# Two orders on VectorE in the first block: when a weight tile's low part is made, and where the ELU's maximum stands

## The chip, the cores and the metric

The kernel runs on one core of a Trainium2 chip. The metric is the device time of one execution in microseconds. The engines speak of themselves as in the profile: PE is the tensor engine's matmuls, PEld its weight loads, DVE is VectorE, ACT is ScalarE, POOL is GpSimd, SP is SyncE, which here issues nearly all transfers.

## The reference

Inputs: q, k, v of 4 x 8 heads x 768 tokens x 64, eight memory keys and values per head, and six weight matrices, handed over as 64-bit floats in two 32-bit words each.

```python
for each chunk of 32 queries:                     # keys: 8 of memory, 16 left, 32 own, 8 right
    scores = (q_c @ k_full.T) / sqrt(64)
    a = exp(scores - max(scores)); a = a / (sum(a) + 1e-9)
    out[chunk] = a @ v_full
x = out as 3072 tokens x 512
h = x @ w_in                                      # 512 -> 2048
g = where(h > 0, h, exp(min(h, 0)) - 1)           # ELU
x = g @ w_out                                     # 2048 -> 512
a, b = x @ w1, x @ w2                             # 512 -> 1024 each
y = ((a * b) @ w3) @ w_out2                       # 1024 -> 1024 -> 512
```

## The kernel before, in words

The tokens are worked on in eight blocks of 384. Attention goes in 24 groups G of 128 queries, three to a block. The first layer and its ELU go in 16 tiles per block: n counts (block, tile), so n = 0 to 15 is the first block. Every large product is made of three matmuls on split operands: high x high, high x low, low x high (`mm3`, L123 to L126), where the high part is a rounded copy (ScalarE) and the low part the remainder (VectorE).

The first block carries more than the later ones: while it runs, the 32 weight tiles of w_in and w_out are brought in, converted and split for the first time. `Feed` does this, one job per weight tile, in steps. Step i issues, for different jobs:

- on ScalarE `hi_of` (L172, the high part of job i-2's tile) and `rebase` (L159, the first pass over the raw words of job i);
- on VectorE `shift` (L163) and `low` (L167) of job i-1, then `lo_of` (L175, the low part of job i-2's tile);
- on SyncE the loads of raw words for later jobs (L140, L148): there are four raw buffers, and four more for the first 16 jobs. A buffer comes free when `low` has read it.

The intermediate f tiles have four buffers, so `rebase` of job i writes where job i-4 was last read by `lo_of`. `until(i)` runs steps until job i is complete.

Five steps run before the loop (the `f` letters in START, between the attention of groups 0 to 2). Then iteration n < 16 issues in this order; each engine takes its own instructions in the order of issue (the schedule is written out by hand):

1. `mm_h(n)`: 12 matmuls into one of two banks that alternate with n; it must wait until `elu_max(n-2)` has read that bank.
2. `elu_hi(n-1)` (ScalarE, L559), a feed step, `elu_lo(n-1)` (VectorE, L563).
3. `at_step`: the attention work of slot 2n.
4. `elu_exp(n)`: two ScalarE passes (L549, L550).
5. `x()`: `mm_x(n-2)` (12 matmuls that read elu_lo's result), a feed step, `at_step` of slot 2n+1.
6. `elu_max(n)` (VectorE, L555).

A slot holds steps of a group's attention: turn (L305 to L317), scores (L329), max (L346, L347, then the exponential L348 on ScalarE), sum (L354 to L357), norm (L366, two instructions), flip (L377), values (L388), out (split, L120 on ScalarE and L121 on VectorE). For groups 3, 4 and 5 the odd slots that hold VectorE work are those of n = 2 and 7 (sum), 3 and 8 (flip), 4 and 9 (out), 12 (max) and 13 (norm).

The job order is w_in 0, 1, 2, then w_out and w_in in turn, so w_in tile n is job 2n-2 (n of 2 and more) and w_out tile n-2 is job 2n-1.

The functions that the diff touches, with their callers:

Of the kernel before, what the change touches and what calls it, by code (L numbers as in the profile page):

```python
# [19 lines left out]
def tile_kernel(  # L20
# [41 lines left out]
    FF1 = w_in.shape[1] // P  # L62
# [124 lines left out]
    class Feed:  # L187
# [16 lines left out]
        def step(self):  # L204
            i = self.at
            self.load(i + 1)
            if i - 2 == first_late:
                end_early()
            if 0 <= i - 2 < len(self.jobs):
                self.jobs[i - 2].to = W[self.jobs[i - 2].slot]  # L210
            self.do(i - 2, hi_of)
            self.do(i - 1, shift, low)
            self.do(i - 2, lo_of)
            self.do(i, rebase)
            self.at += 1
            self.load(max(min(i + RAWS + SPARE, SPARE_JOBS), i + RAWS))

        def until(self, i):
            while self.at - 3 < i:
                self.step()  # L220


# [306 lines left out]
    def at_step():  # L529
        store_next()  # L530
        for _, _, fn, arg in sorted(slots.pop(slot_at[0], ()), key=lambda x: x[:2]):
            fn(arg)
        slot_at[0] += 1
# [204 lines left out]
    with tc.manual_schedule():  # L738
        def weight(i):
            if i < FF1:  # L740
                return Job((raw_cols, w_in, i), slot=i)
            return Job((raw_rows, w_out, i - FF1, 0), slot=i)

        jobs, due = [], {}
        order = sorted(range(2 * FF1), key=lambda i: i if i < FF1 else i - FF1 + 2)
        for i in order:
            due[i] = len(jobs)
            jobs.append(weight(i))
        first_late = min(due[i] for i in LATER)
        feed = Feed(jobs)  # L750

        load_qk(0)
        make_identity(nc, ident)
        nc.gpsimd.memset(front, 0.0)
        nc.gpsimd.memset(vw[0:LEFT, 0], 0.0)
        for c in range(NCG):
            for s in range(2):
                nc.gpsimd.memset(odd[c * CH:(c + 1) * CH, s], float(c % 2 == s))
        feed.load(1)
        load_qk(1)  # L760
        feed.load(2)
        load_v(0)
        load_qk(2)
        load_v(1)
        feed.load(3)
        load_v(2)
        feed.load(5)
        one = dict(t=at_turn, u=at_first, s=at_scores, m=at_max, z=at_sum, n=at_norm, p=at_flip, v=at_values, o=at_out, k=load_qk, w=load_v)
        for what in START.split():
            if what == "f":  # L770
                feed.step()
            else:
                one[what[0]](int(what[1]))
        early_psum.close()
        psum_x = ctx.enter_context(tc.tile_pool(name="psum_x", bufs=1, space=PSUM))
        for i in range(KT):
            PS[i] = psum_x.tile([P, 512], F32, name=f"bank{i}")
        NH = NB * FF1
        for n in range(NH + 2):
            j, f, at, last = seq[n] if n < NH else (NB, n - NH, n - NH, False)  # L780
            first = at < 2 and n >= 2
            if j == NB - 1 and f == 0:
                store_next()
                mid_ctx.close()
                at_ctx.close()
                late = ctx.enter_context(tc.tile_pool(name="late", bufs=1, side="right"))
                more = [late.tile([P, 2, 2, TB], F32R, name=f"xc{i}") for i in range(3)]
                left.append({})
                for i, what in enumerate(LEFTS[:4]):
                    left[0][what] = [xhl[i // 2][:, r, i % 2 * 2:i % 2 * 2 + 2, :] for r in range(2)]  # L790
                for i, what in enumerate(LEFTS[4:]):
                    left[0][what] = [more[i][:, r] for r in range(2)]
            if n == FF1:
                feed.until(len(feed.jobs) - 1)
                raw_ctx.close()
                mid_ctx = ExitStack()
                pools["raw"] = mid_ctx.enter_context(tc.tile_pool(name="raw2", bufs=2, side="right"))
                pools["st"] = mid_ctx.enter_context(tc.tile_pool(name="st_p", bufs=2, side="right"))
                mid_load(2)

            def x():
                if n >= 2:
                    if n < FF1 + 2:
                        feed.until(due[FF1 + seq[n - 2][1]])
                    mm_x(n - 2)
                    if at == 1 and n < NH:
                        store_x1(j - 1)
                if n < FF1:
                    feed.step()
                at_step()  # L810

            if first:
                x()
            if n < NH:
                if j == 0:
                    feed.until(due[f])
                mm_h(n)
            spread = n < FF1
            if 1 <= n <= FF1:
                elu_hi(n - 1)  # L820
            if spread:
                feed.step()
            if 1 <= n <= FF1:
                elu_lo(n - 1)
            if n < NH and not spread:
                elu_exp(n)
            at_step()
            if spread:
                elu_exp(n)
            if FF1 < n < NH:  # L830
                elu_lo(n - 1)
            if not first:
                x()
            if n < NH:
                elu_max(n)
            if n < NH and not spread:
                elu_hi(n)
                if n == NH - 1:
                    elu_lo(n)
            if n >= NH - FF1:  # L840

                free = [f] if n < NH else []
                if n >= NH - FF1 + 2:
                    free.append(FF1 + n - 2 - (NH - FF1))
                for slot in free:
                    keep_free(slot)
            if j == NB - 1:
                if f == 4:
                    load_x1(0)
                if f == 8:  # L850
                    left_step(0, 0)
                if f == 10:
                    left_step(0, 1)
        store_x1(NB - 1)
        wq_places()
        load_wq(0, range(3))
        for i in range(2, len(LEFTS)):
            left_step(0, i)
        load_x1(1)
        for half in range(2):  # L860
            for c in range(FF2):
                for i in range(KT):
                    mm_wc(half, c, i)
                    if c == FF2 - 1:
                        keep_wc(half, i)
                if half:
                    if c == 0:
                        load_wq(0, [3])
                    if c in (1, 2, 3):
                        load_wq(1, [c - 1])  # L870
                    if c == 3:
                        load_wq(1, [3])
                    if c in (4, 5, 6):
                        load_wq(2, [c - 4])
                    if c == 7:
                        load_wq(2, [3])
        w_ctx.close()
        end = ctx.enter_context(tc.tile_pool(name="end", bufs=1))
        more = [end.tile([P, 2, 2, TB], F32R, name=f"xd{i}") for i in range(len(LEFTS))]
        left.append({what: [t[:, r] for r in range(2)] for what, t in zip(LEFTS, more)})  # L880
        e_f.update(enumerate([eg_p.tile([P, TB], F32, tag="eg", name="eg") for _ in range(2)] + [end.tile([P, TB], F32, name=f"e{i}") for i in range(4)]))
        gq.extend([g_p.tile([P, 2, TB], F32R, tag="g", name="g") for _ in range(3)] + [end.tile([P, 2, TB], F32R, name="g3")])
        NA = NPAIR * FF2
        for n in range(NA + 1):
            p, f = divmod(n, FF2)

            def behind(t, n=n, p=p, f=f):
                if t == 0 and n < NA and p + 1 < NPAIR and f >= 1:
                    left_step(p + 1, f - 1)
                if n >= 1:  # L890
                    mm_o(n - 1, t)

            def stored(t, p=p, f=f, n=n):
                if n >= 1 and f == 0:
                    store_out(p - 1, t)

            mm_step(n, n == NA, {t: lambda t=t: behind(t) for t in range(2 * GPB)}, stored)
            if n < NA:
                if p + 2 < NPAIR and f == FF2 - 1:
                    load_x1(p + 2)  # L900
                load_wq(n + FOLD)
# [30 lines left out]
```

## Time and profile before

| | |
|---|---|
| median of 3 runs | 1092.84 us (1092.37 to 1093.17) |
| the profiled execution | 1092.9 us, span 1091.1 us |
| PE, PEld busy, share of the span | 96%, 91% |
| DVE, ACT busy | 53%, 42% |
| mean granted clock of TensorE | 0.983 |
| transfers | 180.40 MB, 165 GB/s |

The shares are means over stages. The first block is roughly the stretch from 33 to 133 us; its 17th tile, n = 16, starts the second block. Matmuls are pipelined: the busy time of PE counts ends that are modelled, and the start-to-start distance says how fast it goes. In a timeline row the first number is the start in us from the span's start, the second the duration; the bracket at the end gives the idle time before the instruction and what ended it.

### The profile page before, as it was taken

Reading aid. Unit: us, or ns where it says so; the run is one execution under the profiler, and the core shown is the slowest. Engines: PE = TensorE matmul, PEld = TensorE weight load, DVE = VectorE, ACT = ScalarE, POOL = GpSimd, SP = SyncE. Lnnn points to the kernel's source line nnn. Section 1 sums busy time; section 2 is a strip of 40 time slices with the busy share of each in tenths; the row PEclk is TensorE's granted clock in tenths of the full one; section 3 lists DMA queues with packets and bytes.
Section 4 is the critical chain, followed back from the end, with each engine's and each line's share of the span. In section 5 each row is a group of like instructions: output and inputs, shape, how many; then the busy total and the mean of one; then the engine's idle time right before and its main releaser. Section 6 shows DMA issues by size and latency. Waiting matters only on the chain.

```text
span 1091.1 us, 20849 instructions
## 1 busy us (share of the span) xinstructions
PE 1049.1 (96%) x8528; PEld 991.6 (91%) x8528; DVE 581.9 (53%) x1080; ACT 458.5 (42%) x965; POOL 1.7 (0%) x16
## 2 busy tenths in 40 slices
PE   4788899999999999999999999999999999999998
PEld 3688899999999999999999999789999999999997
DVE  4898656666566567665565334134443444443333
ACT  3676455455555455555454443022232223222222
POOL 0000000000000000000000000000000000000000
PEclk8799999999999999999999999999999999999999
DMA  8956356555454466455351765455466466555521
GB/s 193 299 142 189 99 152 176 154 168 163 144 169 134 137 177 187 126 162 172 105 155 44 244 245 172 137 182 169 143 212 234 155 211 223 156 170 186 186 85 58
DMA packets 170090, 180.40 MB, mean 165 GB/s; under 512 B 101388, under 2 KB 140300, under 8 KB 169996
## 3 DMA queue, kind: packets, MB, share of 16 engines
q1 hardware_dynamic: 168956, 178.81, 53.5%
q8 instruction: 67, 1.10, 0.4%
q10 hardware_dynamic: 1040, 0.26, 0.1%
q14 instruction: 27, 0.22, 0.1%
HBM read 139.20 MB, written 39.85 MB: 164 GB/s over the span
## 4 chain that ended last, share of the span: by engine, by line
PE 86%; DVE 6%; ACT 5%; issue 1%; DMA 1%; SPq 0%; ACTq 0%; DVEq 0%
PE bank L124 18%; PE bank L125 18%; PE bank L126 18%; PE bank L672 7%; PE bank L673 7%; PE bank L671 7%; PE banks L388 2%; PE banks L126 2%; PE banks L125 2%; PE banks L124 2%; PE banks L329 1%; DVE w L175 1%; PE banks L305 1%; ACT w L172 1%; ACT f L159 1%
## 5 line engine op out<-in xcount | busy, mean ns | idle before, releaser
L124 PE MATMUL bank<-xhl,w 128*128 128x384 f32 x512 | 178.2, 348 | 10.6 <-DVE eg L555 9.8
L124 PE MATMUL bank<-g,w 128*128 128x384 f32 x512 | 175.7, 343 | 0.0
L125 PE MATMUL bank<-xhl,w 128*128 128x384 f32 x512 | 173.8, 339 | 0.9 <-DVE xhl L121 0.9
L126 PE MATMUL bank<-xhl,w 128*128 128x384 f32 x512 | 173.8, 339 | 0.0
L125 PE MATMUL bank<-g,w 128*128 128x384 f32 x512 | 171.7, 335 | 0.0
L126 PE MATMUL bank<-g,w 128*128 128x384 f32 x512 | 171.6, 335 | 0.0
L559 ACT CAST g<-eg 128x384 fp32r<-128x384 f32 x128 | 66.1, 517 | 111.9 <-DVE eg L555 111.5
L124 PEld LDWEIGHTS bank<-xhl,w 128*128 128x128 f32 x512 | 97.6, 191 | 14.7 <-DVE eg L555 11.5
L555 DVE SCALAR_TENSOR_TENSOR eg<-eg,bank 128x384 f32<-128x384 f32 x128 | 70.1, 548 | 55.7 <-ACT eg L550 55.7
L455 DVE TENSOR_TENSOR e<-bank,e 128x384 f32<-128x384 f32 x64 | 35.7, 558 | 118.9 <-PE bank L673 76.6
L125 PEld LDWEIGHTS bank<-xhl,w 128*128 128x128 f32 x512 | 97.9, 191 | 1.3 <-DVE xhl L121 1.3
L549 ACT ACTIVATE eg<-bank 128x384 f32<-128x384 f32 x128 | 62.8, 491 | 85.1 <-PE bank L126 85.0
L126 PEld LDWEIGHTS bank<-xhl,w 128*128 128x128 f32 x512 | 97.9, 191 | 0.0
L124 PEld LDWEIGHTS bank<-g,w 128*128 128x128 f32 x512 | 96.6, 189 | 1.1
L125 PEld LDWEIGHTS bank<-g,w 128*128 128x128 f32 x512 | 96.7, 189 | 0.2 <-DVE g L563 0.2
L126 PEld LDWEIGHTS bank<-g,w 128*128 128x128 f32 x512 | 96.4, 188 | 0.0
L719 ACT CAST g<-e 128x384 fp32r<-128x384 f32 x64 | 29.7, 511 | 145.7 <-DVE e L455 145.7
L563 DVE TENSOR_TENSOR g<-eg,g 128x384 fp32r<-128x384 f32 x128 | 70.7, 552 | 16.9 <-ACT g L559 16.9
L672 PE MATMUL bank<-xd,w 128*128 128x384 f32 x224 | 75.8, 338 | 0.0
L673 PE MATMUL bank<-xd,w 128*128 128x384 f32 x224 | 75.6, 337 | 0.0
L671 PE MATMUL bank<-xd,w 128*128 128x384 f32 x224 | 74.9, 334 | 0.0
L550 ACT ACTIVATE eg<-eg 128x384 f32<-128x384 f32 x128 | 67.3, 526 | 4.1
(141 smaller groups left out, 1824.2 us busy)
## 6 DMA issues: line engine op xcount, KB each, us to landing
w<-wqd SPq DMA_DIRECT2D x96, 512.0 KB
raw<-in_moe_w_dram SPq DMA_DIRECT2D x32, 512.0 KB
wqd<-st SPq DMA_DIRECT2D x24, 512.0 KB
raw<-in_moe_w_out_dram SPq DMA_DIRECT2D x20, 512.0 KB
w3d<-st SPq DMA_DIRECT2D x16, 512.0 KB
w<-w3d SPq DMA_DIRECT2D x16, 512.0 KB
w<-wqd SPq DMA_DIRECT2D x32, 256.0 KB
raw<-in_moe_w_in_dram SPq DMA_DIRECT2D x12, 512.0 KB
```

The costliest lines, as they stand in the source:

```text
L124: mm(o, lhsT=w_hi, rhs=x_hi, start=start, stop=False)
L125: mm(o, lhsT=w_hi, rhs=x_lo, start=False, stop=False)
L126: mm(o, lhsT=w_lo, rhs=x_hi, start=False, stop=stop)
L455: nc.vector.tensor_tensor(out=o, in0=a, in1=b, op=op)
L549: nc.scalar.activation(e, h_t[n], AF.Relu, scale=-1.0)
L550: nc.scalar.activation(e, e, AF.Exp, scale=-1.0)
L555: nc.vector.scalar_tensor_tensor(out=e, in0=e, scalar=-1.0, in1=h_t.pop(n), op0=ALU.add, op1=ALU.max)
L559: nc.scalar.copy(g_t[n][:, 0, :], eg_t[n])
L563: nc.vector.tensor_tensor(out=g[:, 1, :], in0=eg_t.pop(n), in1=g[:, 0, :].bitcast(F32), op=ALU.subtract)
L671: mm(o, lhsT=args[0], rhs=args[2], start=start and i == 0, stop=False, skip_group_check=more)
L672: mm(o, lhsT=args[0], rhs=args[3], start=False, stop=False, skip_group_check=more)
L673: mm(o, lhsT=args[1], rhs=args[2], start=False, stop=i == 1, skip_group_check=more)
```

## The change

In the feed, the low part of a weight tile is issued one step later than before, and ahead of `shift` and `low` instead of behind them; `until` counts one step more. In the loop, for n < 16, `elu_max(n)` is issued inside `x()`, between the feed step and the attention of slot 2n+1, instead of after it. For n of 16 and more nothing changes.

```diff
@@ Feed.step
             self.do(i - 2, hi_of)
+            self.do(i - 3, lo_of)
             self.do(i - 1, shift, low)
-            self.do(i - 2, lo_of)
             self.do(i, rebase)
@@ Feed.until
-            while self.at - 3 < i:
+            while self.at - 4 < i:
                 self.step()
@@ x(), in the loop over n
                 if n < FF1:
                     feed.step()
+                    elu_max(n)
                 at_step()
@@ the end of an iteration
             if not first:
                 x()
-            if n < NH:
+            if FF1 <= n < NH:
                 elu_max(n)
```

## Rows read from the trace of the kernel before

**Rows 1.** Busy time of each engine, 42 to 124 us (windows view).

```profile
42.00:124.00 82.00, 69.84 (x667) 66.02 (x666) 71.80 (x135) 56.46 (x118) 0.00 (x0) 0.95 0.61 174
```

**Rows 2.** Waits of VectorE, 42 to 124 us (total us, times, longest).

```profile
DVE w L175 <- ACT w L172: 7.0, 7, 1.4
DVE xhl L121 <- ACT xhl L120: 0.5, 2, 0.2
```

**Rows 3.** The tensor engine's waits for the maximum, 42 to 124 us (same view).

```profile
PE bank L124 <- DVE eg L555: 9.8, 4, 3.1
```

**Rows 4.** VectorE's groups by line, 42 to 124 us: the maximum.

```profile
L555 DVE SCALAR_TENSOR_TENSOR eg<-eg,bank 128x384 f32<-128x384 f32 x14 | 7.6, 542 | 0.0
```

**Rows 5.** VectorE in order of time, 109 to 126 us (start, us; idle before).

```profile
109.00 0.69 DVE L175 TENSOR_TENSOR w<-f,w 128x512 fp32r<-128x512 f32 x1 [1.42 <-ACT w L172]
...
120.07 0.69 DVE L167 SCALAR_TENSOR_TENSOR f<-raw,f 128x512 int32<-128x512 int32 x1
120.68 0.68 DVE L175 TENSOR_TENSOR w<-f,w 128x512 fp32r<-128x512 f32 x1
121.28 1.29 DVE L366 TENSOR_TENSOR e<-e,rc 128x512 f32<-128x512 f32 x2
122.48 0.55 DVE L555 SCALAR_TENSOR_TENSOR eg<-eg,bank 128x384 f32<-128x384 f32 x1
...
124.74 0.55 DVE L563 TENSOR_TENSOR g<-eg,g 128x384 fp32r<-128x384 f32 x1
125.21 1.24 DVE L377 STREAM_TRANSPOSE pT<-e 128x1024 f32<-128x1024 f32 x1
```

**Rows 6.** The tensor engine in order of time, 123 to 133 us.

```profile
123.08 0.57 PE L124 MATMUL bank<-xhl,w 128*128 128x384 f32 x1 [2.38 <-DVE eg L555]
...
126.93 1.16 PE L388 MATMUL banks<-pT,vw 64*64 64x64 f32 x64
...
132.73 0.44 PE L124 MATMUL bank<-xhl,w 128*128 128x384 f32 x1
```

**Rows 7.** The tensor engine's largest wait from 133 us to the end.

```profile
PE banks L305 <- DVE st L175: 2.2, 6, 0.4
```

**Rows 8.** VectorE in order of time, iterations 0 to 2.

```profile
43.12 0.69 DVE L175 TENSOR_TENSOR w<-f,w 128x512 fp32r<-128x512 f32 x1 [1.14 <-ACT w L172]
...
46.38 0.69 DVE L175 TENSOR_TENSOR w<-f,w 128x512 fp32r<-128x512 f32 x1 [1.05 <-ACT w L172]
...
50.05 0.69 DVE L167 SCALAR_TENSOR_TENSOR f<-raw,f 128x512 int32<-128x512 int32 x1
50.78 0.69 DVE L175 TENSOR_TENSOR w<-f,w 128x512 fp32r<-128x512 f32 x1
...
56.08 0.68 DVE L354 TENSOR_REDUCE sm<-e 128x8 f32<-128x512 f32 x1
...
57.33 0.55 DVE L555 SCALAR_TENSOR_TENSOR eg<-eg,bank 128x384 f32<-128x384 f32 x1
```

**Rows 9.** ScalarE in order of time, iterations 0 to 2.

```profile
42.05 0.52 ACT L550 ACTIVATE eg<-eg 128x384 f32<-128x384 f32 x1
42.48 0.60 ACT L172 CAST w<-f 128x512 fp32r<-128x512 f32 x1
...
45.30 0.54 ACT L559 CAST g<-eg 128x384 fp32r<-128x384 f32 x1
45.71 0.64 ACT L172 CAST w<-f 128x512 fp32r<-128x512 f32 x1
...
54.40 0.52 ACT L550 ACTIVATE eg<-eg 128x384 f32<-128x384 f32 x1
```

**Rows 10.** SyncE issues the raw tile of job 24.

```profile
88.94 0.37 SPq L140 DMA_DIRECT2D raw<-in_moe_w_in_dram  x1
```

**Rows 11.** ScalarE reads that tile.

```profile
97.53 0.67 ACT L159 ACTIVATE f<-raw 128x512 f32<-128x512 f32 x1
```

**Rows 12.** One raw tile's transfer, from the chain of waits (start, us).

```profile
59.01 3.29 DMA raw<-in_moe_w_in_dram
```
## The prediction

> **What bounds the kernel now.** I read the page first: over the whole span the tensor engine is busy nearly throughout, VectorE half of the time. That mean hides the first block, so the second view was the table of windows over 42 to 124 us, in which the feed of weights runs. There VectorE is busy 71.80 of 82.00 us and has the highest share of the engines [rows 1]. Third, the waits: in this stretch VectorE stands still 7.0 us, in 7 places, for the high part of a weight tile (w L172) before it can make the low part (w L175), and 0.5 us for attention's high part [rows 2]; the tensor engine stands still 9.8 us, in 4 places, for the maximum (eg L555) [rows 3]. The maximum itself never waited: idle before its 14 instructions is 0.0 [rows 4]. So the chain is: VectorE goes through its list in order, loses time at low parts whose high parts are late, and arrives late at elu_max; the next-but-one mm_h, which needs that bank, is late by as much. The last of these places is the hinge: elu_max(13) starts at 122.48 [rows 5], mm_h(15) starts right after it at 123.08, after 2.38 us of waiting [rows 6]. From there to mm_h(16) at 132.73 the tensor engine hardly pauses, and from 133 us to the end its largest wait adds up to 2.2 us, in pieces of 0.4 at most [rows 7]. What mm_h(15) gains is therefore not taken back later by an idle tensor engine: nothing downstream has a time of its own to wait for.
>
> **The sum: how much earlier is elu_max(13)?** I count what stands ahead of it on VectorE, before and after.
>
> *The waits for the high part.* After the change the low part in step i belongs to job i-3, whose high part was issued one step before; it finds it done. The 7 waits go: 7.0 us [rows 2]. Beside them are small delays below the resolution of that view: where nothing delays it, L175 starts 0.61 us after L167 (120.07 and 120.68, [rows 5]); in the second step of an iteration the two are 0.73 apart (50.05 and 50.78, [rows 8]), and I counted ten such pairs in the stretch: 10 x 0.12 = 1.2 us. The 0.5 us at attention's out [rows 2] stand in slots of n = 4 and 9, where elu_max (0.54 us, [rows 4]) now comes first and fills them.
>
> *What moves behind it.* In iteration 13 the odd slot holds norm, two instructions that take 1.20 us from start to start (121.28 to 122.48, [rows 5]); elu_max(13) now goes ahead of them. And with the low part one step later, one L175 fewer has been issued by then: 0.60 us (120.68 to 121.28, [rows 5]).
>
> Together 7.0 + 1.2 + 0.5 + 1.20 + 0.60 = 10.5 us.
>
> *What waits instead.* Behind the first seven places stands, in the new order, an instruction that also needs ScalarE: elu_max needs L550, elu_lo needs L559. Each of these sits one instruction ahead of the high part on ScalarE (L550 42.05, L172 42.48: 0.43; L559 45.30, L172 45.71: 0.41, [rows 9]), and the old job's low part, now in front, fills 0.60 more. So of a wait w about w - 1.03 is left: 0.11 of 1.14, 0.02 of 1.05 [rows 8], 0.39 of 1.42 [rows 5], and 0.7 over all seven. This holds while ScalarE keeps its distance to VectorE. Where it does not, the rest is larger: at 46.38 ScalarE comes from mm_h(0) and the copies of a turn. mm_h(0) starts some 0.6 us earlier (one low part fewer stands ahead of attention's last out before the loop), while VectorE has by then gained 1.14, so that about 0.5 us stays. There are three turns in the block; with half of that at the two others I take 0.7 + 0.8 = 1.5 us. The bounds: 0 if ScalarE follows wholly; 4.0 if the three turns keep their waits (1.05 [rows 8], 1.42 [rows 5] and a like one of 0.94) and 0.6 of the others stays. I stay nearer to the low end, because ScalarE is busy only 56.46 of 82 us [rows 1] and is itself mostly waiting for the maximum.
>
> elu_max(13) and mm_h(15) are earlier by 10.5 - 1.5 = 9.0 us.
>
> *Behind the hinge.* mm_h(15) is followed by the values of group 5 (L388). Before, they started at 126.93, which is 4.45 after elu_max(13) began and right behind mm_h(15)'s matmuls [rows 5, 6]. After, flip is late next: from elu_max's start 0.46 for it, norm 1.20, one low part 0.60, elu_lo 0.47 (124.74 to 125.21), flip 1.24 [rows 5], so 4.0 in all. If mm_h(15) runs as slowly as before (3.85 us up to the values, [rows 6]) the values start 4.45 after as well, otherwise up to 0.45 earlier. I take 0.2. Sum: 9.0 + 0.2 = 9.2 us.
>
> **Edits that I cost at nothing.** *Weights that are complete one step later.* mm_h(n) reads job 2n-2, whose low part is now made in step 2n+1; it waits anyway for elu_max(n-2), issued behind step 2n+2. mm_x(n-2) reads job 2n-1, made in step 2n+2, and waits anyway for elu_lo(n-2), behind step 2n+3. Neither can become the later one. *f tiles held one step longer.* rebase of job i now needs the low part of step i-1; but it stands behind the high part of job i-2, and that needs `low` of the same step, which VectorE makes after that low part. *until* asks for 35 steps at n = 16, and 37 have been issued. *SyncE* keeps its order; its raw loads wait for `low`, and come earlier with it.
>
> **The wait that is added.** elu_max(n) now stands ahead of attention's VectorE work in iterations 2, 3, 7, 8, 12 and 13, and that work, the next low part, shift and low stand behind its wait for L550; scores and values on the tensor engine wait for them. In iteration 2 L550 ended at 54.92 [rows 9] and elu_max began at 57.33 [rows 8]: 2.4 us of room, of which the move takes the 1.25 us that sum stood ahead of it (from 56.08, [rows 8]). 1.15 us is left, so I cost it at 0 beyond the rest above.
>
> One more look at whether VectorE's waits can be won back at all. The gaps of about 1.1 us in front of L175 [rows 8] stand beside pairs of the same kind that follow in 0.61 [rows 5], so a wait on another engine comes on top of the instructions' own pace. The Trainium skill speaks against the change here: VectorE: DVE Perf Modes, "The DRAIN you can't avoid", says that the flush behind each instruction sets the pace, and that taking out the semaphores between chained instructions saved nothing in its measurement. By that rule the sum would be 0, since the number of instructions stays; the trace does not agree where the awaited engine is another one.
>
> **The rivals.**
>
> *A. ScalarE takes over.* If the low part in front does not help, because VectorE arrives early by what it gained, then only the 0.43 of each wait goes: 7.0 - 7 x 0.43 = 4.0 stays, and so do the ten small delays and the 0.5. The gain is 10.5 - 4.0 - 1.7 = 4.8, the time 1088.1. For it: the same ScalarE list serves both. Against: its room above.
>
> *B. The number of instructions sets VectorE's pace.* 135 start in 82.00 us [rows 1], 0.607 each, about what L175 takes where nothing delays it; the change leaves their number as it is. Then the gaps would reappear elsewhere, and the time would be 1092.9. Against: the gaps stand at one kind of instruction only, and the maximum, which needs ScalarE too, has none [rows 4].
>
> *C. The raw tiles come too late.* Job 24's was issued at 88.94 [rows 10] and read at 97.53 [rows 11], 8.6 us later; one transfer took 3.29 [rows 12]. A pace that is faster by 9.2 of 82 us leaves 7.6. If transfers took over 8 us under load, jobs 16 to 31 would keep the old pace, half of the gain would go: about 1088.3. Against: 3.29.
>
> *D. Slower.* elu_max stops VectorE in front of attention. It decides from the point at which L550 comes more than 1.15 us later, relative to VectorE, than before. At 3.2 us later in all six iterations 6 x 2.05 = 12.3 us are lost against 10.5 gained: 1094.7. For it: VectorE gains time that ScalarE has to follow. Against: no idle time at all before the maximum so far [rows 4].
>
> **How the numbers follow.** The profiled execution took 1092.9 us (span 1091.1), 0.06 above the median of the runs, which I neglect. 1092.9 - 9.2 = 1083.7. Chances: forecast 0.72 (its own range 1082.3 to 1085.6: 7.3 to 10.6 gained, from a rest of 0 to 3.4), A 0.14, B 0.05, C 0.04, D 0.05. The range 1082.0 to 1088.4 takes in the forecast, A and C and leaves out B, D and the tails. Faster by over 0.2% (what a measurement can tell from no change): forecast, A and C, 0.90; within it B, 0.05; slower D, 0.05.
>
> **What would show it.** Right: in the changed trace VectorE's wait for L172 at L175 is gone from the waits of the first block, the tensor engine's 9.8 us for the maximum shrink to 1 or 2, mm_h(15) starts near 114 and mm_h(16) near 123.5 us; from there all is as before, shifted. A new wait of about 1 us at elu_lo(0), and waits of the values for flip of 1 to 2 us, belong to the forecast. Wrong: waits of L555 for L550 or of L563 for L559 that add up to 4 us (A), idle ScalarE at L159 for a transfer (C), or attention's instructions late behind L555 (D). If VectorE needs as long as before from 42 us to elu_max(13), B holds; if mm_h(16) is early by 9 and the end is not, the first paragraph was wrong about what comes behind.

## The result, and the profile after

The changed kernel takes 1083.38 us (median of 6 runs, 1083.16 to 1083.60) against 1092.91 of the kernel before in the same comparison: a ratio of 0.9914, with a 95% interval of 0.9903 to 0.9924, or 9.5 us less. Predicted were 1083.7 us, between 1082.0 and 1088.4. Its profiled execution has a span of 1081.4 us against 1091.1, so 9.7 us of difference lie in the two traces that are read here.

The windows view of the changed kernel, from 42 us to 115 us, answers to [rows 1]. The columns are the window, its length, the busy time and instructions of PE, PEld, DVE, ACT and POOL, the granted clock as a share of full speed, the share of the transfer engines and GB/s.

```profile
42.00:115.00 73.00, 66.64 (x667) 64.02 (x666) 70.10 (x135) 56.35 (x117) 0.00 (x0) 0.98 0.68 200
```

The same 135 VectorE instructions and the same 667 matmuls fit into 73 us instead of 82. VectorE is busy 96% of them, before it was 88%.

What VectorE waited for in that window (waits view: total us, times, longest), and the groups of its low parts, `low`, shift, the maximum and elu_lo, against [rows 2] and [rows 4]:

```profile
DVE g L563 <- ACT g L559: 1.0, 1, 1.0
DVE eg L555 <- ACT eg L550: 0.5, 1, 0.5
```

```profile
L175 DVE TENSOR_TENSOR w<-f,w 128x512 fp32r<-128x512 f32 x27 | 18.4, 681 | 0.0
L167 DVE SCALAR_TENSOR_TENSOR f<-raw,f 128x512 int32<-128x512 int32 x20 | 13.9, 693 | 0.7
L163 DVE TENSOR_SCALAR f<-f 128x512 int32<-128x512 int32 x26 | 10.9, 419 | 0.0
L555 DVE SCALAR_TENSOR_TENSOR eg<-eg,bank 128x384 f32<-128x384 f32 x14 | 7.7, 548 | 0.6 <-ACT eg L550 0.5
L563 DVE TENSOR_TENSOR g<-eg,g 128x384 fp32r<-128x384 f32 x13 | 7.2, 551 | 1.0 <-ACT g L559 1.0
```

The 27 low parts no longer wait at all (the last number of a group is its idle time); the 7.0 us are gone. In their place stand one wait of elu_lo(0) and one of elu_max(11), 1.5 us in all.

The tensor engine's waits in the same window, against [rows 3], and its hinge in order of time, against [rows 6]:

```profile
PE banks L388 <- DVE pT L377: 3.8, 2, 2.3
PE bank L124 <- DVE eg L555: 1.0, 1, 1.0
PE banks L329 <- ACT front L317: 0.9, 1, 0.9
PE bank L125 <- DVE g L563: 0.6, 1, 0.6
```

```profile
113.62 0.44 PE L124 MATMUL bank<-xhl,w 128*128 128x384 f32 x1 [1.04 <-DVE eg L555]
...
117.05 1.28 PE L388 MATMUL banks<-pT,vw 64*64 64x64 f32 x64 [1.05 <-DVE pT L377]
...
122.65 0.42 PE L298 MATMUL banks<-ident,head 16*128 16x16 f32 x4
...
123.00 0.44 PE L124 MATMUL bank<-xhl,w 128*128 128x384 f32 x1
```

The wait for the maximum fell from 9.8 us to 1.0. The values wait 3.8 us for flip instead, and 1.05 more just behind the window. mm_h(15) starts 9.46 us earlier than before, the values of group 5 9.88, mm_h(16) 9.73. From there everything is shifted: the tensor engine's largest wait from 123 us to the end is the old one, 2.2 us.

### The profile page after: what moved, and what is told of

Read it like the earlier page. It is cut to its first block, busy times and chain, and to the rows that moved or that the text cites. A ratio compares the mean times of both kernels' runs of the same rounds, so it can differ in the third digit from the quotient of the medians.

```text
span 1081.4 us, 20852 instructions
## 1 busy us (share of the span) xinstructions
PE 1045.0 (97%) x8528; PEld 988.6 (91%) x8528; DVE 580.3 (54%) x1080; ACT 458.7 (42%) x965; POOL 1.7 (0%) x16
## 4 chain that ended last, share of the span: by engine, by line
PE 87%; DVE 7%; ACT 3%; issue 2%; DMA 1%; SPq 0%; ACTq 0%; DVEq 0%
PE bank L124 18%; PE bank L125 18%; PE bank L126 18%; PE bank L672 7%; PE bank L673 7%; PE bank L671 7%; PE banks L388 2%; PE banks L126 2%; PE banks L125 2%; PE banks L124 2%; PE banks L329 1%; DVE w L175 1%; PE banks L305 1%; PE banks L307 1%; DVE eg L555 1%
## 5 line engine op out<-in xcount | busy, mean ns | idle before, releaser
L555 DVE SCALAR_TENSOR_TENSOR eg<-eg,bank 128x384 f32<-128x384 f32 x128 | 70.1, 548 | 56.3 <-ACT eg L550 56.1
L563 DVE TENSOR_TENSOR g<-eg,g 128x384 fp32r<-128x384 f32 x128 | 70.6, 551 | 17.9 <-ACT g L559 17.9
```

What stands on the lines that cost most here:

```text
L555: nc.vector.scalar_tensor_tensor(out=e, in0=e, scalar=-1.0, in1=h_t.pop(n), op0=ALU.add, op1=ALU.max)
L563: nc.vector.tensor_tensor(out=g[:, 1, :], in0=eg_t.pop(n), in1=g[:, 0, :].bitcast(F32), op=ALU.subtract)
```

## The experiments

Each was timed against the kernel before; the changed kernel's 1083.38 is from its own comparison, so differences to it below 0.5 us or so are read with care.

**The low part alone.** elu_max stays at the end of the iteration.

```diff
             self.do(i - 2, hi_of)
+            self.do(i - 3, lo_of)
             self.do(i - 1, shift, low)
-            self.do(i - 2, lo_of)
@@ Feed.until
-            while self.at - 3 < i:
+            while self.at - 4 < i:
```

> The first part of the change alone: low part one step later and in front, elu_max at its old place. Theory (VectorE's waits for the high part are the main cost, the order at the end the smaller one): removed 7.0 + 1.2 us and one L175 (0.6), left about 1.5, so 7.0 to 7.5 us faster than before, about 1085.6; L175 has no wait for L172, and the tensor engine still waits some 3 us in all for eg L555 in iterations 2, 7 and 13, where attention stands ahead of the maximum. Rival (the bank's wait is what counts, so the place of elu_max is the change): at most 2 us faster, 1091. Rival A (ScalarE takes over): 4 us faster, 1089.

1084.01 us (1083.67 to 1085.31), ratio 0.9923, interval 0.9911 to 0.9936: 8.7 us faster than before, more than the 7.5 expected. The tensor engine around the hinge:

```profile
115.60 0.44 PE L124 MATMUL bank<-xhl,w 128*128 128x384 f32 x1 [2.25 <-DVE eg L555]
...
117.90 1.27 PE L388 MATMUL banks<-pT,vw 64*64 64x64 f32 x64
```

mm_h(15) is 7.48 us earlier than before, as expected. But from its start to the values it takes 2.30 us here and took 3.85 before [rows 6]. The windows view of the kernel before (first), and of this one (second), shows why: the clock of the tensor engine.

```profile
123.10:127.00 3.90, 3.90 (x16) 3.64 (x20) 2.76 (x4) 1.99 (x5) 0.00 (x0) 0.56 0.02 4
```

```profile
115.60:118.00 2.40, 2.40 (x16) 2.15 (x20) 2.40 (x4) 1.93 (x4) 0.00 (x0) 1.00 0.00 0
```

Before, mm_h(15) ran at 0.56 on average, most of it at the lower of the two levels (0.50, 1.2 of 2.4 GHz), after a wait of 2.38 us; here it ran at 1.00 after a wait of 2.25. So 1.55 us of the gain stand behind the hinge in these two traces, not in VectorE's list. One execution of each kernel has a trace; how often the clock falls at this place is not shown.

**The maximum alone.** The low part stays as before.

```diff
                 if n < FF1:
                     feed.step()
+                    elu_max(n)
                 at_step()
@@
-            if n < NH:
+            if FF1 <= n < NH:
                 elu_max(n)
```

> The second part of the change alone: elu_max in front of the second attention step, low part as before. Theory: VectorE's 7 us of waits stay, the maximum gains the 1.2 us of norm at iteration 13 and some of the waits, so 2 to 2.5 us faster than before, about 1090.5. Rival (the bank's wait is what counts): 7 to 9 us faster, 1084 to 1086. Rival D (the maximum stops attention): slower than before. If the two parts were independent, their gains would add up to 9.5.

1090.12 us (1089.69 to 1090.55), ratio 0.9976, interval 0.9967 to 0.9985: 2.5 us faster than before. Its VectorE keeps the waits:

```profile
DVE w L175 <- ACT w L172: 7.0, 7, 1.4
```

Its tensor engine around the hinge:

```profile
120.20 0.44 PE L124 MATMUL bank<-xhl,w 128*128 128x384 f32 x1 [1.17 <-DVE eg L555]
...
123.63 1.28 PE L388 MATMUL banks<-pT,vw 64*64 64x64 f32 x64 [1.05 <-DVE pT L377]
```

The bank's wait is thus the symptom: an earlier maximum shortens it (9.8 to 3.8 us in this kernel), and yet three quarters of the gain do not come, because VectorE's list still holds the seven waits. The gains of the two parts, 8.7 and 2.5, add up to 11.2, the change has 9.5: they overlap by 1.7. In the traces, mm_h(15) is 7.48 and 2.88 us earlier alone and 9.46 together, so 0.9 of the overlap is there already; behind it the values gain 1.55 and 0.42 more alone, and 0.42 together.

**Where they overlap.** The maximum of iteration 13 alone goes back behind norm.

```diff
                     feed.step()
-                    elu_max(n)
+                    if n != FF1 - 3:
+                        elu_max(n)
...
-            if FF1 <= n < NH:
+            if FF1 <= n < NH or n == FF1 - 3:
```

> The changed kernel with the maximum of iteration 13 alone at its old place, behind norm. Theory from the prediction (each of the two edits at the hinge counts in full: norm's 1.20 us): 1.0 us slower, 1084.4, mm_h(15) 1.2 later. Rival (norm and flip, which the values of group 5 wait for, come earlier by what the maximum comes later, so the hinge's 1.20 us is mostly given back): within 0.4 us of 1083.4. If the rest of the second edit (iterations 0 to 12) is worth something, this kernel stays faster than the one with the first edit alone, 1084.0.

1083.31 us (1083.17 to 1084.93): no difference from the changed kernel. mm_h(15) is late, the values are not:

```profile
114.97 0.44 PE L124 MATMUL bank<-xhl,w 128*128 128x384 f32 x1 [2.25 <-DVE eg L555]
...
117.27 1.27 PE L388 MATMUL banks<-pT,vw 64*64 64x64 f32 x64
...
122.83 0.42 PE L298 MATMUL banks<-ident,head 16*128 16x16 f32 x4
```

The 1.35 us by which mm_h(15) comes later (114.97 against 113.62) are 0.22 at the values and 0.18 at the turn behind it. What norm costs in front of the maximum, flip gains. So at the hinge the second edit is worth next to nothing once the first is in. What it adds to the first alone (1084.01 to 1083.38) then lies in the other iterations: mm_h(16) starts at 123.81 in the kernel with the low part alone and at 123.18 here.

**Late, but behind.** The low part one step late, at its old place in the step.

```diff
             self.do(i - 2, hi_of)
-            self.do(i - 3, lo_of)
             self.do(i - 1, shift, low)
+            self.do(i - 3, lo_of)
```

> Both parts, but the low part, one step late, stands behind shift and low as before, not in front. Theory: lateness takes the wait away, the place in front only fills about 0.6 us ahead of the instructions that still need ScalarE; so most of the gain stays: 1.0 to 2.0 us slower than the changed kernel, 1084.4 to 1085.4, with VectorE's waits for ScalarE at shift, elu_max and elu_lo a little longer. Rival (the place in front does it): 5 us or more slower than the changed kernel, 1088 or more. Rival (the place is nothing): within 0.5 us of 1083.4.

1084.34 us (1083.94 to 1085.02): 0.96 above the changed kernel, just below the lower edge of what was expected. Lateness carries the gain; standing in front is worth about 1 us. The place shows in the waits of its VectorE, 42 to 122 us: `shift` now waits for rebase, which the low part in front had covered; elu_lo and elu_max wait about as long as in the changed kernel.

```profile
DVE f L163 <- ACT f L159: 1.6, 3, 0.5
DVE g L563 <- ACT g L559: 1.0, 2, 0.6
DVE eg L555 <- ACT eg L550: 0.7, 2, 0.5
```

**More and less VectorE work.** One more pass, or the shift left out, in each of the 32 jobs of the changed kernel; shift_none is a shift by 0 over the same tile.

```diff
-            self.do(i - 1, shift, low)
+            self.do(i - 1, shift, shift_none, low)
```

> The changed kernel with one more VectorE pass in each of the 32 feed jobs (a shift by 0 over the f tile, 0.455 us from start to start, 14.6 us in all; the result is unaffected). Theory (VectorE's list is the bound of the first block, with under 2 us of idle time): 11 to 14 us slower, 1094 to 1097. Rival B (its instructions are not what the time hangs on) or a tensor engine that bounds the block: under 5 us slower, below 1088.

1095.49 us (1095.38 to 1095.70): 12.1 us slower for 14.6 us of work. VectorE is the bound of the block, also after the change; both rivals of this run, which expected under 5 us, fall.

```diff
-            self.do(i - 1, shift, low)
+            self.do(i - 1, low)
```

> The changed kernel without the shift of the feed (14.6 us less VectorE work in the first block; the weights of the first two layers come out as other numbers). It measures what the next bound is. Theory: VectorE gets lighter than the tensor engine, whose own work in the stretch is some 75 us and who waits for 8 us in the changed kernel; so about half of it comes through: 5 to 7 us faster, 1076.5 to 1078.5. Rival (VectorE is still the bound): 13 to 15 us faster, 1069. Rival (another engine bounds already): no change.

1076.52 us (1076.39 to 1076.56): 6.9 us faster for 14.6 us less. About half comes through, as expected. Then the other two engines take over as limits; its windows view, 42 to 108 us, and its VectorE's waits from 42 to 112 us:

```profile
42.00:108.00 66.00, 63.73 (x661) 61.86 (x661) 60.35 (x111) 56.43 (x118) 0.00 (x0) 1.00 0.75 216
```

```profile
DVE eg L555 <- ACT eg L550: 4.3, 6, 1.5
DVE g L563 <- ACT g L559: 2.8, 3, 1.5
```

The tensor engine is busy 97% of the stretch, and VectorE waits 7 us for ScalarE.

**More ScalarE work.** rebase twice in each job.

```diff
-            self.do(i, rebase)
+            self.do(i, rebase, rebase_again)
```

> The changed kernel with one more ScalarE pass in each of the 32 feed jobs (rebase twice, 0.57 us from start to start, 18 us in all; the result is unaffected). Theory (ScalarE has room: about 20 us of the changed block it waits for the maximum and for attention): most is hidden, 2 to 5 us slower than the changed kernel, 1085.5 to 1088.5, the rest as waits of VectorE for L549/L550 and L559. Rival A (ScalarE is the bound after the change): 15 to 18 us slower, about 1100.

1090.07 us (1089.89 to 1090.40): 6.7 us slower for 18 us of work, between the two answers. The stretch of 42 to 120 us, and VectorE's longest waits in it (in this kernel L166 is shift, L566 elu_lo, L558 elu_max):

```profile
42.00:120.00 78.00, 68.04 (x667) 64.30 (x665) 69.95 (x134) 72.55 (x142) 0.00 (x0) 0.97 0.66 188
```

```profile
DVE f L166 <- ACT f L162: 3.3, 6, 0.6
DVE g L566 <- ACT g L562: 1.5, 2, 1.0
DVE eg L558 <- ACT eg L553: 1.2, 1, 1.2
```

ScalarE is now the busiest engine, 93%. So rival A does not describe the change (ScalarE is busy 77% there), but the room is smaller than the idle time says: of 18 us some 11 were hidden. VectorE waits 6.0 us for ScalarE in these three groups, against 1.5 in the changed kernel, and more than half of it at shift, which the expectation did not name. The theory took all of ScalarE's idle time for room. A likely reason why it is not, argued and not tested: the changed kernel's ScalarE stands still 10.1 us in 6 places for the maximum and 5.5 in 3 for attention, while the added pass of 0.57 comes in every step.

**The low part on GpSimd.** An attempt to take 19 us off VectorE; lo_pool is lo_of with nc.gpsimd.tensor_tensor.

```diff
-            self.do(i - 3, lo_of)
+            self.do(i - 3, lo_pool)
```

> The changed kernel with the low part of the 32 weight tiles of the first block computed by GpSimd instead of VectorE. Theory (VectorE's list bounds the first block, 70.1 of 73 us busy in the changed kernel): 32 x 0.60 = 19 us less on VectorE, but the tensor engine and ScalarE are close behind, so about 6 us faster than the changed kernel, 1077.4, if one GpSimd instruction takes under 2.4 us and does not slow VectorE. Rival (GpSimd is slower than a step, 2.2 us, or takes VectorE's memory port): slower than 1083.4, several us at 3 us an instruction. Rival B (another engine sets the pace): no change.

1095.72 us (1095.00 to 1096.09), slower than both kernels. One GpSimd instruction takes 1.43 us, which would fit; but VectorE's own become longer. Groups of the trace (line, engine, operation | busy, mean ns): GpSimd, then VectorE from 42 to 122 us.

```profile
L180 POOL TENSOR_TENSOR w<-f,w 128x512 fp32r<-128x512 f32 x32 | 45.8, 1432 | 80.4 <-ACT w L172 66.2 <-DVE eg L560 10.1 <-DVE g L568 4.1
```

```profile
L167 DVE SCALAR_TENSOR_TENSOR f<-raw,f 128x512 int32<-128x512 int32 x19 | 18.2, 956 | 0.7
L163 DVE TENSOR_SCALAR f<-f 128x512 int32<-128x512 int32 x26 | 16.4, 630 | 1.8 <-ACT f L159 1.7
L568 DVE TENSOR_TENSOR g<-eg,g 128x384 fp32r<-128x384 f32 x13 | 11.5, 888 | 0.5 <-ACT g L564 0.4
...
L560 DVE SCALAR_TENSOR_TENSOR eg<-eg,bank 128x384 f32<-128x384 f32 x13 | 7.1, 546 | 1.8 <-ACT eg L555 1.8
```

L568 is elu_lo and L560 is elu_max in this kernel. elu_lo takes 888 ns instead of 551, `low` 956 instead of 693, shift 630 instead of 419; elu_max, with one operand in a bank, stays at 546. These means mix two cases. In order of time, two `low`, each beside one GpSimd instruction:

```profile
50.18 0.69 DVE L167 SCALAR_TENSOR_TENSOR f<-raw,f 128x512 int32<-128x512 int32 x1
50.32 1.70 POOL L180 TENSOR_TENSOR w<-f,w 128x512 fp32r<-128x512 f32 x1 [0.46 <-ACT w L172]
...
68.07 1.29 POOL L180 TENSOR_TENSOR w<-f,w 128x512 fp32r<-128x512 f32 x1 [1.29 <-ACT w L172]
68.17 1.73 DVE L167 SCALAR_TENSOR_TENSOR f<-more,f 128x512 int32<-128x512 int32 x1
```

Where `low` starts first it keeps its 0.69 us, and GpSimd's takes 1.70; where GpSimd starts first, it takes 1.29 and `low` ends 0.54 us after it. So it is with every `low` from 42 to 122 us that meets a GpSimd instruction: the six that start first keep 0.69 us, the eight that start second take 1.65 to 1.76. The rival that VectorE's memory port is taken fits this; the trace shows the order of the two, not the port.

**A faster version.** The values of group 5, and what follows from them, one slot later, behind mm_x(13).

```diff
-            put(s0 + at, fn, G)
+            put(s0 + at + (G == 5 and fn in (at_values, at_out)), fn, G)
```

> The changed kernel, with the values and the out of group 5 alone one slot later (behind mm_x(13) instead of ahead of it). In the changed kernel the tensor engine stands still 1.05 us in front of these values, for flip. Theory (behind elu_max(13) the tensor engine's order sets the end; mm_x(13) has its operands by then): about 1.0 us faster than the changed kernel, 1082.4, and the wait at L388 near 117 us gone. Rival (mm_x(13) or the second block's first product then waits as long): no change, 1083.4. Rival (the out of group 5 comes too late for the next turn and mm_h(16)): slower, up to 1 us.

1082.14 us (1081.93 to 1082.24), ratio to before 0.9905, interval 0.9890 to 0.9919: 1.2 us less than the changed kernel, and no run of the one overlaps one of the other. From 105 to 122 us its tensor engine never stops:

```profile
105.00:122.00 17.00, 17.00 (x157) 16.35 (x156) 14.50 (x28) 8.82 (x21) 0.00 (x0) 1.00 0.25 64
```

With one feed step less ahead of the hinge as well:

```diff
                 if n < FF1:
-                    feed.step()
+                    if n != FF1 // 2:
+                        feed.step()
                     elu_max(n)
```

> The changed kernel with the values of group 5 one slot later, and without the feed step in x() of iteration 8, so that every later feed step comes half an iteration later and one of them (1.7 us of VectorE) falls behind elu_max(13). Theory (VectorE bounds the block up to there, its list is shorter by one step): up to 1.7 us faster than the kernel with the later values alone, but the tensor engine is busy nearly throughout from 105 us on there, so about 0.6 us, 1081.5. Rival (weights now come too late for mm_h or mm_x): slower than 1082.1. Rival (the tensor engine bounds already): 1082.1.

1081.43 us (1081.12 to 1081.57), ratio 0.9899, interval 0.9882 to 0.9915: the fastest, 11.1 us below the 1092.56 of before in its comparison. So 0.7 of the 1.7 us of VectorE work comes through. The reason expected, a tensor engine that is busy throughout behind 105 us, is not in this trace:

```profile
111.79 0.44 PE L124 MATMUL bank<-xhl,w 128*128 128x384 f32 x1 [1.04 <-DVE eg L555]
115.12 0.44 PE L125 MATMUL bank<-g,w 128*128 128x384 f32 x1 [0.79 <-DVE g L563]
```

elu_max(13) starts 1.82 us earlier than with the later values alone (111.18 against 113.00), and the tensor engine waits 1.83 us in the two places. In the trace of that kernel it waited for nothing there, but had run mostly at the lower clock from 88 to 92 us (0.57 on average), which it does not here (1.00). Where the other 1.0 us went stays open.

## Why the prediction was right

*The bound.* VectorE's list in order set the first block. Adding work to it costs 12.1 us of 14.6; the part of the change that removes its waits gave 8.7 of the 9.5 us alone, 1.55 of them through the clock behind the hinge.

*The waits for the high part.* Counted in the traces as start-to-start distance beyond an undelayed pair, from L167 of job 5 (at 41.28) to elu_max(13), the kernel before loses 9.4 us to ScalarE and the changed one 2.1. Predicted were 8.7 (7.0 + 1.2 + 0.5) and a rest of 1.5. Both terms are short by 0.6 to 0.7 us, and the difference came out right, 7.3 against 7.2, because the two errors cancel; that was luck. The first is short because a reported gap of 1.14 us is a loss of 1.23: without a wait the next instruction starts before the end of the previous one (0.61 against a duration of 0.69). The rest is larger at three maxima that come 0.1 us late, and at elu_max(11), 0.53; elu_lo(0) lost 1.07, where I had taken 0.5 and, in what would show it, about 1:

```profile
43.40 0.69 DVE L167 SCALAR_TENSOR_TENSOR f<-more,f 128x512 int32<-128x512 int32 x1
...
45.08 0.56 DVE L563 TENSOR_TENSOR g<-eg,g 128x384 fp32r<-128x384 f32 x1 [0.99 <-ACT g L559]
```

*What moves behind the maximum.* The 1.8 us, norm and one low part, were read rightly: from job 5's L167 to elu_max(13) it is 81.2 us before and 72.0 after, without those delays 71.76 and 69.84, so 1.92 apart. At mm_h(15) norm's 1.20 us count, at the end hardly: the kernel with the maximum of iteration 13 at its old place is as fast. There mm_h(15) runs at full clock and the values start 2.90 us after elu_max(13) (114.37 and 117.27); in the changed kernel flip holds them back until 4.03 after. Before, mm_h(15) ran mostly at the lower clock and the values came 4.45 after. So norm's 1.20 us come through against the kernel before because its mm_h(15) was slow. The prediction read that slowness from the row and named flip's 4.0, but it did not see that the two edits share this gain. The 4.03 brings 0.42 behind the hinge where I took 0.2.

*The sum.* mm_h(15) is 9.46 us earlier, predicted 9.0; of the 0.46, 0.22 were there before the block began (the last `shift` before the two edits part the lists starts at 32.79 instead of 33.01), and no part of the change explains them. mm_h(16) is 9.73 earlier, predicted 9.2, and the median 9.5 lower. The forecast's own range does not follow from its terms: with a rest of 0 to 4.0, the stated bounds, the gain is 6.7 to 10.7 us, not 7.3 to 10.6; nothing hangs on it.

*The edits at nothing, and the rivals.* No wait of ScalarE at rebase, no wait of the tensor engine for a weight in either trace. Rival A's sign was 4 us of waits at L555 and L563; 1.5 came. Rival C's transfers were not late. Rival D's point was not reached: elu_max waited 0.5 us in all, in iteration 11, where no attention stands behind it. What came instead is the other wait that was named, that of the values for flip, and larger than the 1 to 2 us named: 2.28, 1.48 and 1.05 us for the three groups. The first two stand where VectorE's list is the bound. Rival B: the number of instructions stayed and the block became 9.7 us shorter. The Trainium skill's rule in VectorE: DVE Perf Modes, "The DRAIN you can't avoid", that semaphores between chained VectorE instructions cost nothing, does not reach to waits on another engine: VectorE's for ScalarE are 7.5 us in the trace before and 1.5 after.

*What the prediction did not see.* That the two parts overlap by 1.7 us, in the traces mostly through the clock and flip: alone, the first part is worth 8.7 and not the 7.0 to 7.5 that the same terms gave.

## What to carry to other kernels

When one engine's list sets a stage, look for the instruction that waits for a partner issued in the same step, and let it serve the job before: the wait goes, at the price of holding a buffer one step longer, and what it cost is read from start-to-start distances, which say more than the reported gaps. Moving a releasing instruction forward is worth only as much as the next one in that list can wait. And before work goes from VectorE to GpSimd, look at where both find their operands.

## What the runs showed of the hardware

GpSimd and VectorE block each other in many pairs of instructions: the one that starts second ends only after the first has ended. Beside GpSimd's tensor_tensor, the mean of elu_lo (128x384, two SBUF sources) went from 551 to 888 ns, of `low` (128x512, two) from 693 to 956, of shift (128x512, one) from 419 to 630. It does not hold for every instruction in SBUF. The sum's reduction (one SBUF source) started 0.1 us before GpSimd's instruction in all three places, and neither became longer: 0.68 us and 1.29 to 1.30. elu_max, with one source in a PSUM bank, kept 0.55 us where it started second. The Trainium skill gives a rule in SBUF — State Buffer, "SBUF: two separate sides": GpSimd and VectorE share a pair of ports as an exclusive lock, which a VectorE instruction needs when it has two SBUF inputs or runs in a two-port mode, and whichever starts first keeps it for the whole instruction. The trace agrees for `low` and elu_lo; which mode shift ran in is not in it.

The tensor engine's clock fell to its lower level at the hinge after a wait of 2.38 us in the kernel before, and not after one of 2.25 at the same place in two of the experiments. The length of the wait alone does not decide it. Group 3's values started at 61.45 us after a wait of 2.28 both in the changed kernel (first) and in the one with the values of group 5 later (second); right behind them the clock was 0.50 in the one and 1.00 in the other:

```profile
62.00:64.00 2.00, 2.00 (x58) 1.88 (x51) 1.97 (x4) 1.72 (x4) 0.00 (x0) 0.50 0.04 8
```

```profile
62.00:64.00 2.00, 2.00 (x55) 1.93 (x47) 1.97 (x4) 1.72 (x4) 0.00 (x0) 1.00 0.13 30
```
